# Moving the selection matrix and the combine matrix's two parts of a fused attention and soft-MoE kernel

## Chip, cores and metric

The kernel runs on one core of one Trainium2 chip. The metric is device time in microseconds (us) of one launch; lower is better. Engines are named as in the profile: PE (TensorE matmul), PEld (its weight loads), ACT (ScalarE), DVE (VectorE), POOL (GpSimd) and SP (the engine that issues the DMAs).

## What is computed

Three layers follow each other. Causal attention with a decay (4 batches, 8 heads, 576 positions, 64 per head) gives `x` of 2304 rows by 512. A soft MoE makes 32 slots out of all rows, sends them through 8 experts (4 slots each) and combines the 32 slot outputs back into rows. A second MoE of 4 experts works on all rows, weighted by given probabilities.

```python
logits = x @ phi                               # 2304 x 32
d = softmax(logits, axis=0); slot_input = d.T @ x
for e in range(8):                             # 4 slots each
    h = np.maximum(slot_input[e] @ w1[e], 0.0)
    slot_out[e] = h @ w2[e]
c = softmax(logits, axis=1)
x = c @ slot_out                               # c: the combine matrix
for e in range(4):                             # second MoE
    h = np.maximum(x @ m1[e], 0.0)
    out += p[:, e:e + 1] * (h @ m2[e])
```

## The kernel before

**Stages.** Attention runs over 16 pairs of heads to some 200 us. Then the last softmax (to 209.7), then layer one of the eight slot experts (`layer1`, L767, to 224), then layer two (`layer2`, L793, to 239), then the preparation of the second MoE (L985 to L1035), then 36 blocks of 256 rows (4 experts by 9 blocks, L1137). From L814 on the order on PE, ACT, DVE and POOL is the program's own order (`manual_schedule`); in the attention stage only PE's order is written by hand (L526) and the other engines' order is the planner's. Each engine runs its own queue in order.

**The stage in question.** `layer2_last` (L802) does the last slot expert in two halves into another bank, and DVE adds each half to `orow`, which ACT has copied out of the accumulated bank (L991, after `layer2(6)`). PE turns `orow` into `so_t` by matmuls with `i4` (L1000), DVE copies it (L1001), and `g_make` (L970) multiplies it by the first layer `m1` of expert 0 (L974). The result is split in a high and a low part (`gh`, `gl`) and `g_spread` (L883) spreads it by matmuls with `sel` into `gs`. `sel` is a constant 0/1 matrix (one wide ACT copy at L865, eight small ones at L869). `pieces` (L896) multiplies `gs` by the transposed combine matrix `c4t`; thus slot outputs and rows meet only there.

**The combine matrix.** `cn` holds the softmax of each row over the 32 slots, for 4 batches by 5 row groups. `c4_rep(b)` (L697) makes for each batch (and once for the fifth groups, b = 4) a tile `c4` of four copies: ACT rounds `cn` into `chi` (L702) and copies `chi` to places 0 and 2 (L704); POOL writes `cn - chi` to places 1 and 3 (`c4_low`, L709). PE transposes `c4` (`c4_tr`, L714) and ACT copies it to `c4t` (`c4_hi`, L719).

**The second MoE's weights.** `m2` of an expert comes as four DMAs of 512 KB into `raws`; pieces 0 and 2 early (L823), pieces 1 and 3 last (L828). Half of each 256-column tile (chunks 0 to 2) is in pieces 0 and 2, the other (chunks 2 to 4) in 1 and 3. Each tile needs a high part by ACT (`w_hi`, L757) and a low part by POOL (`w_lo`, L763): four plain ones (B00, B10, B01, B11) and four sums T1 to T4 that POOL makes first (`w_sum`, L744; T3 and T4 overwrite B01 and B00). Block 0 is done directly with the plain tiles (`direct`, L1076, L1091), after ACT and DVE have written its two parts (`hi_d` L909, `lo_d` L913, which take turns). All later blocks use seven products (`product`, L1057, L1071) with parts made by DVE, ACT and POOL (`a_sum` L960, `s_hi` L964, `s_lo` L968) and their results taken by DVE (`take`, L1052 and L1054). `PRE0` (L1111) is a table of which part is issued after which step of block 0 or 1.

**Weight buffers.** SP loads all expert weights in one fixed order (`stream`) of 512 KB pieces: 4 into `ring`, 17 into `ringb`, 14 into `ringc` (`NB`, L46), 6 in place of attention tiles, 6 into `post` (L559) and `NQ` = 4 into `post2` (L682), which lies where `xnp` and a part of `wk` (the tail of the attention, closed at L681) were. Then two pieces of `m2` once `layer1(0)` has released `ring`, four pieces of the stream after each of `layer1(1)` to `layer1(4)`, and one after `layer1(5)`, into `ringb` (L825).

Of the kernel before, what the change touches and what calls it, by code (L numbers as in the profile page):

```python
# [10 lines left out]
F32R = mybir.dt.float32r  # L11
# [23 lines left out]
def soft_moe_kernel(tc, a, out):  # L35
# [3 lines left out]
    def f32(ap):  # L39
        return ap.bitcast(F32)  # L40

    NQ = 4
    E = mybir.EngineType
    SE = [{'a': nc.scalar, 'd': nc.vector}[x] for x in "ad"]
    WU = 5
    NB = (17, 14)  # L46
    ND = 1
    with ExitStack() as top:
# [634 lines left out]

        eo = top.enter_context(tc.tile_pool(name="eo", bufs=2, side="right"))
        qx.close()

# [7 lines left out]

        c4_ps, c4_in = {}, {}

        def c4_rep(b):  # L697
            src = cn[:64, :, 4] if b == B else cn[:, b, 0:4]
            r = src.shape[0]
            c4 = c4p.tile([r, 4, 4, 32], F32, tag="c4f" if b == B else "c4", bufs=1 if b == B else 4, name=f"c4_{b}")  # L700
            chi = c4p.tile([r, 4, 32], F32R, tag="chi", bufs=5, name=f"chi_{b}")
            act.copy(chi, src)  # L702
            two_of = lambda x: x[:, :, None, :].to_broadcast([r, 4, 2, 32])
            act.copy(c4[:, :, 0:4:2], two_of(f32(chi)))  # L704
            c4_ps[b] = c4
            c4_in[b] = (c4[:, :, 1:4:2], two_of(src), two_of(f32(chi)))

        def c4_low(b):
            pool.tensor_tensor(*c4_in[b], op=ALU.subtract)  # L709

# [103 lines left out]
        man = ExitStack()  # L814
        man.enter_context(tc.manual_schedule(engines={E.PE, E.Activation, E.DVE, E.Pool}))
        for e in range(E1):
            if e == 4:
                hidden(0)
            layer1(e)
            if e == 0:  # L820
                raws[0] = ring.tile([128, 4096], F32, tag="w", name="ring_m2")
                for i in (0, 2):
                    load_w(raws[0][:, 1024 * i:1024 * i + 1024], 1, stream.index(("m2", 0, i)))  # L823
            elif e < 6:
                load_w(ringb[0], 4 if e < 5 else 1)  # L825
            if e == 5:
                for i in (1, 3):
                    load_w(raws[0][:, 1024 * i:1024 * i + 1024])  # L828
            if e == 4:
                turn(0)  # L830
                slots(0)
                slots(1)
# [12 lines left out]
        so_t = c4tp.tile([128, DC, 32], F32, name="so_t")  # L845
        sel = c4tp.tile([128, 4, 2, 128], F32R, name="sel")
        c4tp.tile([128, 8], F32, name="pad2")
# [6 lines left out]
        for x in ("T1", "T2"):  # L854
            w_sum(0, x, 0, 2)
        for x in ("B00", "B10", "B01", "B11"):
            w_hi(0, x, act, 0, 2)
            w_lo(0, x, pool, 0, 2)
        slots(5)
        layer2(5)  # L860
        w_hi(0, "T2", act, 0, 2)
        w_hi(0, "T1", act, 0, 2)
        for b in (0, 1, 2, 3, B):
            c4_rep(b)
        act.activation(sel, ident[:, None, None, 0:1].to_broadcast([128, 4, 2, 128]), AF.Copy, scale=0.0)  # L865
        for jq in range(4):
            for i in range(2):
                r = slice(32 * jq, 32 * jq + 32)
                act.copy(sel[r, jq, i, 64 * i:64 * i + 64].rearrange("p (a s) -> p a s", a=2),  # L869
                         i4[r, None, :].to_broadcast([32, 2, 32]))  # L870
        c4_low(0)
        w_sum(0, "T3", 0, 2)
        w_sum(0, "T4", 0, 2)
        c4_low(1)
        c4_low(2)
        w_lo(0, "T2", pool, 0, 2)
        c4_low(3)
        c4_low(B)
        w_lo(0, "T1", pool, 0, 2)
        slots(6)  # L880
# [105 lines left out]
        def c4_bank(b):  # L986
            return ops.tile([128, DM], F32, tag="o", name=f"ct_{b}")
# [18 lines left out]
        gg = g_make(0, bank(0, 0)[:, 0:256], range(2, DC))  # L1006
        w_hi(0, "B00", act, 2, 4)
        w_lo(0, "B00", pool, 2, 4)
        for b in (1, 2):
# [6 lines left out]
        for hf in range(2):  # L1016
            g_spread(0, *gg, hf)
        w_hi(0, "B10", act, 2, 4)
        w_lo(0, "B10", pool, 2, 4)
        c4_tr(3, c4_bank(3))  # L1020
        pieces(0, 0)
        hi_d(0, 0, 0)
        lo_d(0, 0, 0)
        hi_d(0, 0, 1)
        lo_d(0, 0, 1)
        c4_tr(B, c4_bank(B))
        pieces(0, 1)
        hi_d(0, 1, 0)
        lo_d(0, 1, 0)
        hi_d(0, 1, 1)  # L1030
        lo_d(0, 1, 1)
# [44 lines left out]
        def direct(m):  # L1076
# [3 lines left out]
            for n in range(2):  # L1080
# [29 lines left out]

        PRE0 = {(0, 0): [("hi", "B01", "a", 2, 4), ("lo", "B01", "p", 2, 4)],  # L1111
# [6 lines left out]
        ENG = {"a": act, "d": dve, "p": pool}  # L1118
# [164 lines left out]
```

## Time and profile before

| what | us |
|---|---|
| median of the runs shown (3) | 658.71 |
| lowest, highest | 657.29, 658.84 |
| the profiled execution | 658.35 |
| its span, first to last instruction | 656.6 |

PE is busy for 644.6 us of the span (98%), PEld 576.4 (88%), DVE 482.5 (73%), POOL 420.0 (64%), ACT 355.8 (54%). The mean granted TensorE clock is 0.995 of full speed. An engine's busy time is the union of its instructions; matmuls overlap, so their durations add up to more than the time they take. Idle time of an engine matters only where another one waits for it.

### The profile page before, as it was taken

Reading aid. Unit: us, or ns where it says so; the run is one execution under the profiler, and the core shown is the slowest. Engines: PE = TensorE matmul, PEld = TensorE weight load, DVE = VectorE, ACT = ScalarE, POOL = GpSimd, SP = SyncE. Lnnn points to the kernel's source line nnn. Section 1 sums busy time; section 2 is a strip of 40 time slices with the busy share of each in tenths; the row PEclk is TensorE's granted clock in tenths of the full one; section 3 lists DMA queues with packets and bytes.
Section 4 is the critical chain, followed back from the end, with each engine's and each line's share of the span. In section 5 each row is a group of like instructions: output and inputs, shape, how many; then the busy total and the mean of one; then the engine's idle time right before and its main releaser. Section 6 shows DMA issues by size and latency. Waiting matters only on the chain.

```text
span 656.6 us, 15328 instructions
## 1 busy us (share of the span) xinstructions
PE 644.6 (98%) x5646; PEld 576.4 (88%) x5646; DVE 482.5 (73%) x1330; ACT 355.8 (54%) x868; POOL 420.0 (64%) x384
## 2 busy tenths in 40 slices
PE   8999999999999989999999999999999999999998
PEld 4778788788787449899999999999999999999997
DVE  6889889888885015577678877778876778877774
ACT  7777777777772065533547343547443446444441
POOL 5677777677641195843889663789754589835443
PEclk9999999999999989999999999999999999999999
DMA  5687787787347980213000303000303000011111
GB/s 170 194 246 222 212 265 224 216 255 229 90 167 296 415 351 1 88 42 130 1 1 1 130 1 129 2 0 2 129 1 129 1 1 2 33 46 52 51 48 65
DMA packets 27510, 76.16 MB, mean 116 GB/s; under 512 B 4014, under 2 KB 4654, under 8 KB 27436
## 3 DMA queue, kind: packets, MB, share of 16 engines
q1 hardware_dynamic: 27436, 75.18, 33.9%
q8 instruction: 45, 0.74, 0.5%
q14 instruction: 29, 0.24, 0.1%
HBM read 70.31 MB, written 4.72 MB: 114 GB/s over the span
## 4 chain that ended last, share of the span: by engine, by line
PE 85%; ACT 4%; DVE 3%; POOL 3%; issue 2%; DMA 2%; ACTq 0%; DVEq 0%; POOLq 0%
PE R L1071 27%; PE Q L1071 13%; PE P L1071 7%; PE avb L290 5%; PE pt L273 5%; PE two L902 5%; PE sc L240 3%; PE sc L237 3%; PE sc L224 3%; PE pl L342 2%; PE ava L302 2%; PE pt L264 2%; DMA w<-in_w 2%; PE two L974 1%; PE nat L317 1%
## 5 line engine op out<-in xcount | busy, mean ns | idle before, releaser
L968 POOL TENSOR_TENSOR s<-S,s 128x512 fp32r<-128x512 f32 x140 | 179.8, 1320 | 131.1 <-ACT s L964 131.1
L964 ACT CAST s<-S 128x512 fp32r<-128x512 f32 x140 | 77.2, 619 | 88.7 <-PE Q L1071 51.2
L214 ACT ACTIVATE p<-p,nm 128x256 f32<-128x256 f32 (+2 forms) x144 | 83.3, 580 | 28.6 <-DVE nm L210 27.3
L1071 PE MATMUL R<-wh_T,s 128*128 128x256 f32 x560 | 88.8, 280 | 0.7 <-DVE acc L1054 0.7
L1054 DVE SCALAR_TENSOR_TENSOR acc<-R,dpn,acc 128x256 f32<-128x256 f32 x116 | 56.0, 483 | 34.6 <-PE R L1071 31.0
L934 ACT ACTIVATE a<-two 128x256 f32<-128x256 f32 x70 | 26.9, 384 | 94.9 <-PE two L902 94.5
L1071 PEld LDWEIGHTS R<-wh_T,s 128*128 128x128 f32 x560 | 75.2, 188 | 1.9 <-ACT a L943 1.2
L210 DVE CUSTOM_DVE_ANT_0 p<-sc,maskb 128x256 f32<-128x256 f32 (+2 forms) x144 | 66.9, 489 | 3.2 <-PE sc L224 1.5
L960 DVE SCALAR_TENSOR_TENSOR S<-two,S 128x256 f32<-128x256 f32 x140 | 58.9, 421 | 4.3 <-POOL s L968 1.8
L960 DVE SCALAR_TENSOR_TENSOR S<-two,a 128x256 f32<-128x256 f32 x140 | 58.1, 415 | 3.8 <-POOL s L968 2.2
L191 POOL TENSOR_TENSOR opd<-raw,opd 64x576 fp32r<-64x576 f32 x29 | 42.3, 1459 | 13.9 <-ACT opd L176 12.8
L950 DVE SCALAR_TENSOR_TENSOR q<-two,q 128x512 fp32r<-128x512 f32 x70 | 47.7, 681 | 0.0
L273 PE MATMUL pt<-ident,p 128*128 128x128 f32 x285 | 46.0, 279 | 1.3 <-ACT p L214 0.7
L902 PE MATMUL two<-c4t,gs 128*128 128x256 f32 x288 | 46.5, 284 | 0.0
L237 PE MATMUL sc<-opd 128*128 128x256 f32 (+3 forms) x128 | 46.4, 374 | 0.0
L1071 PE MATMUL Q<-wh_B,s 128*128 128x256 f32 x280 | 43.8, 278 | 1.4 <-DVE acc L1052 1.4
L1071 PE MATMUL R<-wh_T,q 128*128 128x256 f32 x280 | 44.4, 280 | 0.0
L273 PEld LDWEIGHTS pt<-ident,p 128*128 128x128 f32 x285 | 31.4, 140 | 14.8 <-issue 10.4
L1071 PE MATMUL R<-wh_B,a 128*128 128x256 f32 x280 | 44.2, 280 | 0.0
L1071 PE MATMUL R<-wl_T,s 128*128 128x256 f32 x280 | 44.1, 279 | 0.0
L1071 PE MATMUL Q<-wh_T,s 128*128 128x256 f32 x280 | 44.1, 279 | 0.0
L1071 PE MATMUL P<-wh_B,q 128*128 128x256 f32 x280 | 44.0, 279 | 0.0
(279 smaller groups left out, 1626.8 us busy)
## 6 DMA issues: line engine op xcount, KB each, us to landing
w<-in_w SPq DMA_DIRECT2D x54, 512.0 KB
ring<-in_m SPq DMA_DIRECT2D x24, 512.0 KB
raw<-in_k SPq DMA_DIRECT2D x64, 144.0 KB
v<-in_v SPq DMA_DIRECT2D x16, 320.0 KB
out<-acc SPq DMA_DIRECT2D x17, 256.0 KB
raw<-in_q SPq DMA_DIRECT2D x28, 144.0 KB
ring<-in_w SPq DMA_DIRECT2D x4, 512.0 KB
w_opd<-in_w SPq DMA_DIRECT2D x4, 512.0 KB
```

Source lines behind the costliest of these rows:

```text
L191: (dve if h == 0 else pool).tensor_tensor(lo, r, f32(hi), op=ALU.subtract)
L210: dve.tensor_tensor_reduce(out=pt_in[j][:, k0:k0 + n], in0=sc, in1=maskb[:, m0:m0 + n], scale=-SCALE, scalar=nm, op0=ALU.add, op1=ALU.min, ...
L214: act.activation(p, p, AF.Exp, bias=nm, scale=-1.0, accum_out=sums)
L237: pe.matmul(o, lhsT=qa[hh][:, qs], rhs=ka[hh][:, 0:n], start=True, stop=False)
L273: pe.transpose(t[:, i, :], pt_in[j][:, 128 * i:128 * i + 128], ident)
L902: pe.matmul(t[:, j, k], lhsT=gs[e][:, 128 * fc:128 * fc + 128], rhs=c4t[:, nb * BLK:nb * BLK + BLK])
L950: dve.scalar_tensor_tensor(o[:, 1], i, 0.0, f32(o[:, 0]), op0=ALU.max, op1=ALU.subtract)
L960: dve.scalar_tensor_tensor(sv[m, name][:, c], half[m, h][:, :, k, 128 * t:128 * t + 128], 0.0, other, op0=ALU.max, op1=op)
L964: act.copy(tile_of(m, name)[:, 0], sv[m, name])
L968: (eng or pool).tensor_tensor(o[:, 1], sv[m, name], f32(o[:, 0]), op=ALU.subtract)
L1054: dve.scalar_tensor_tensor(o, t, pcol, o, op0=ALU.mult, op1=ALU.add)
L1071: pe.matmul(t, lhsT=a[:, c, :], rhs=w[:, c, :], start=first and x == 0 and c == 0, stop=x == 2 and c == 3, skip_group_check=True)
```

## The change

`sel` and `chi` become tiles of the pool `eo`, which opens before layer one; `chi` is one tile for all batches. Ahead of the layer-one loop ACT rounds `cn` into `chi` in two copies (128 and 64 partitions) and POOL subtracts `chi` from `cn` in place, twice; ACT then makes `sel` there (L865 to L870 go). `c4_rep` becomes two ACT copies for each of its five calls, of `chi` and of the remaining `cn`; `c4_low` and its five POOL instructions go. To make room `post2` gets 2 pieces instead of 4 (`NQ`), `ringb` 19 buffers and `ringc` 12, and the load after `layer1(5)` takes 3 pieces instead of 1. In the preparation of the second MoE the high and low parts of B00, B10 and B01 (chunks 2 to 4) and the sums T1, T2 are issued at other places among the steps of block 0, and `PRE0` is shorter by what went there.

```diff
-    NQ = 4
+    NQ = 2
-    NB = (17, 14)
+    NB = (19, 12)
@@ after load_w(... "post2" ...)
         eo = top.enter_context(tc.tile_pool(name="eo", bufs=2, side="right"))
+        sel = eo.tile([128, 4, 2, 128], F32R, tag="sel", bufs=1, name="sel")
+        chi = eo.tile([128, B, 5, 32], F32R, tag="chi", bufs=1, name="chi")
@@ c4_rep
-            src = cn[:64, :, 4] if b == B else cn[:, b, 0:4]
-            r = src.shape[0]
+            src = [x[:64, :, 4] if b == B else x[:, b, 0:4] for x in (f32(chi), cn)]
+            r = src[0].shape[0]
-            chi = c4p.tile([r, 4, 32], F32R, tag="chi", bufs=5, name=f"chi_{b}")
-            act.copy(chi, src)
-            act.copy(c4[:, :, 0:4:2], two_of(f32(chi)))
+            for i in range(2):
+                act.copy(c4[:, :, i:4:2], src[i][:, :, None, :].to_broadcast([r, 4, 2, 32]))
-        def c4_low(b):
-            pool.tensor_tensor(*c4_in[b], op=ALU.subtract)
@@ ahead of the layer-one loop
+        for p, c in ((128, slice(0, 4)), (64, slice(4, 5))):
+            act.copy(chi[:p, :, c], cn[:p, :, c])
+            pool.tensor_tensor(cn[:p, :, c], cn[:p, :, c], f32(chi[:p, :, c]), op=ALU.subtract)
+        act.activation(sel, ident[:, None, None, 0:1].to_broadcast([128, 4, 2, 128]), AF.Copy, scale=0.0)
+        for jq in range(4):
+            for i in range(2):
+                act.copy(sel[...], i4[...])
@@ in the loop
-                load_w(ringb[0], 4 if e < 5 else 1)
+                load_w(ringb[0], 4 if e < 5 else 3)
@@ between layer2(4) and layer2(6)
+        for x in ("B00", "B10", "B01", "B11", "T2", "T1"):
+            w_hi(0, x, act, 0, 2)
         for x in ("B00", "B10", "B01", "B11"):
-            w_hi(0, x, act, 0, 2)
             w_lo(0, x, pool, 0, 2)
         slots(5)
         layer2(5)
-        w_hi(0, "T2", act, 0, 2)
-        w_hi(0, "T1", act, 0, 2)
         for b in (0, 1, 2, 3, B):
             c4_rep(b)
-        act.activation(sel, ...)   and the eight copies
-        c4_low(0)
-        w_sum(0, "T3", 0, 2)
-        w_sum(0, "T4", 0, 2)
-        c4_low(1)
-        c4_low(2)
-        w_lo(0, "T2", pool, 0, 2)
-        c4_low(3)
-        c4_low(B)
-        w_lo(0, "T1", pool, 0, 2)
+        for x in ("T3", "T4"):
+            w_sum(0, x, 0, 2)
+        for x in ("T2", "T1"):
+            w_lo(0, x, pool, 0, 2)
@@ preparation of block 0
-        w_hi(0, "B00", act, 2, 4)            # stood ahead of c4_tr(1)
-        w_lo(0, "B00", pool, 2, 4)
         for hf in range(2):
             g_spread(0, *gg, hf)
-        w_hi(0, "B10", act, 2, 4)
-        w_lo(0, "B10", pool, 2, 4)
+        w_sum(0, "T1", 2, 4)
+        w_hi(0, "B00", act, 2, 4)
+        w_lo(0, "B00", pool, 2, 4)
         pieces(0, 0)
         hi_d(0, 0, 0)
         lo_d(0, 0, 0)
+        w_hi(0, "B10", act, 2, 4)
+        w_lo(0, "B10", pool, 2, 4)
         hi_d(0, 0, 1)
         lo_d(0, 0, 1)
+        w_sum(0, "T2", 2, 4)
         pieces(0, 1)
         hi_d(0, 1, 0)
         lo_d(0, 1, 0)
+        w_hi(0, "B01", act, 2, 4)
+        w_lo(0, "B01", pool, 2, 4)
         hi_d(0, 1, 1)
@@ PRE0: B01 leaves it, T1 and T2 sums leave it,
-        (0, 1): B11 hi, lo, sums T1 T2;  (0, 3): sums T3 T4;  (0, 4): T2, T1 hi, lo
-        (0, 5): T3 hi;  (0, 6): T4 hi;  (1, 1): T3 lo;  (1, 2): T4 lo
+        (0, 0): B11 hi, lo, sums T3 T4;  (0, 2): T2, T1 hi, lo;  (0, 3): T3 hi, lo
+        (0, 5): T4 hi;  (1, 1): T4 lo
```

## Rows read from the trace of the kernel before

**Rows 1.** The page's 40 slices: granted TensorE clock in tenths of full.

```profile
PEclk9999999999999989999999999999999999999999
```

**Rows 2.** Waits of PE, 230 to 250 and 250 to 275 us: total, times, longest.

```profile
PE two L1000 <- DVE orow L810: 1.9, 1, 1.9
PE two L808 <- DMA w<-in_w: 0.2, 1, 0.2
...
PE Q L1071 <- DVE acc L1052: 1.4, 1, 1.4
```

**Rows 3.** Windows: length; busy of PE, PEld, DVE, ACT, POOL; PEclk; DMA share; GB/s.

```profile
240.00:241.00 1.00, 0.00 (x0) 0.00 (x0) 0.29 (x1) 0.95 (x5) 1.00 (x2) 1.00 1.02 418
241.00:242.00 1.00, 0.81 (x5) 0.82 (x6) 0.46 (x2) 1.00 (x2) 1.00 (x2) 0.76 1.02 418
245.00:246.00 1.00, 1.00 (x15) 0.39 (x8) 0.00 (x0) 0.00 (x0) 1.00 (x2) 0.50 0.00 0
...
272.00:273.00 1.00, 0.29 (x3) 0.08 (x1) 0.24 (x1) 0.00 (x0) 1.00 (x2) 1.00 0.00 0
...
275.00:400.00 125.00, 124.76 (x1088) 122.13 (x1086) 92.63 (x215) 57.52 (x119) 79.38 (x61) 1.00 0.14 52
```

**Rows 4.** Timeline of PE: start, length, instructions, idle before and what ended it.

```profile
209.69 1.93 PE L773 MATMUL two<-ring,si_f 128*32 128x256 f32 x32
...
237.82 1.49 PE L808 MATMUL two<-w,ht 128*32 128x256 f32 x20 [0.23 <-DMA w<-in_w]
...
251.61 0.28 PE L1091 MATMUL d<-wh_B,q 128*128 128x256 f32 x1
```

**Rows 5.** The chain that ended last, in order of time: start, length, what.

```profile
240.71 0.43 DVE orow L810
...
243.58 3.57 PE two L974 x32
```

**Rows 6.** Timeline of ACT, 237 to 253 us.

```profile
237.30 0.40 ACT L704 COPY c<-chi 64x256 f32<-64x256 f32 x1
237.62 1.05 ACT L865 ACTIVATE sel<-ident 128x1024 fp32r<-128x1024 f32 x1
238.70 1.58 ACT L869 CAST sel<-i 32x64 fp32r<-32x64 f32 x8
240.30 0.65 ACT L991 COPY orow<-so_ps 128x256 f32<-128x256 f32 x2
...
243.93 0.62 ACT L757 CAST wh_B<-ring_m 128x512 fp32r<-128x512 f32 x1 [0.42 <-DMA ring_m<-in_m]
...
252.12 1.09 ACT L909 ACTIVATE q<-two 128x512 fp32r<-128x512 f32 x2 [0.76 <-DVE q L913]
```

**Rows 7.** Timeline of POOL, 209 to 273 us.

```profile
209.82 0.48 POOL L671 TENSOR_TENSOR cn<-ce,cs_e 128x160 f32<-128x160 f32 x1 [5.72 <-DVE dps L672]
...
234.96 0.73 POOL L709 TENSOR_TENSOR c<-cn,chi 128x256 f32<-128x256 f32 x1
...
257.57 1.29 POOL L763 TENSOR_TENSOR wl_B<-ring_m,wh_B 128x512 fp32r<-128x512 f32 x1 [0.26 <-ACT wh_B L757]
...
272.69 1.26 POOL L763 TENSOR_TENSOR wl_T<-ring_m,wh_T 128x512 fp32r<-128x512 f32 x1
```

**Rows 8.** Timeline of DVE, just ahead of PE's wait at 273 us.

```profile
272.76 0.42 DVE L960 SCALAR_TENSOR_TENSOR S<-two,S 128x256 f32<-128x256 f32 x1 [0.81 <-POOL s L968]
273.10 0.48 DVE L1052 TENSOR_SCALAR acc<-Q,dpn 128x256 f32<-128x256 f32 x1
```

**Rows 9.** Windows as rows 3, where the weight loads pause and start again.

```profile
210.00:211.00 1.00, 1.00 (x24) 0.58 (x20) 0.74 (x4) 0.00 (x0) 0.30 (x1) 1.00 0.01 4
211.00:212.00 1.00, 1.00 (x24) 0.64 (x20) 0.00 (x0) 0.00 (x0) 0.00 (x0) 1.00 0.56 106
```

**Rows 10.** Waits of SP's DMA queue, 186 to 260 us: total, times, longest.

```profile
SPq L73 <- PE busy L661: 6.0, 1, 6.0
...
SPq L73 <- POOL cn L671: 1.1, 1, 1.1
```

More of the change, by code (lines that the diff above doesn't have):

```diff
@@ L693, in soft_moe_kernel @@
         ops = top.enter_context(tc.tile_pool(name="ops", bufs=4, space=PSUM))
-        c4_ps, c4_in = {}, {}
+        c4_ps = {}
         def c4_rep(b):
-            src = cn[:64, :, 4] if b == B else cn[:, b, 0:4]
-            r = src.shape[0]
+            src = [x[:64, :, 4] if b == B else x[:, b, 0:4] for x in (f32(chi), cn)]
+            r = src[0].shape[0]
             c4 = c4p.tile([r, 4, 4, 32], F32, tag="c4f" if b == B else "c4", bufs=1 if b == B else 4, name=f"c4_{b}")
-            chi = c4p.tile([r, 4, 32], F32R, tag="chi", bufs=5, name=f"chi_{b}")
-            act.copy(chi, src)
-            two_of = lambda x: x[:, :, None, :].to_broadcast([r, 4, 2, 32])
-            act.copy(c4[:, :, 0:4:2], two_of(f32(chi)))
+            for i in range(2):
+                act.copy(c4[:, :, i:4:2], src[i][:, :, None, :].to_broadcast([r, 4, 2, 32]))
             c4_ps[b] = c4
-            c4_in[b] = (c4[:, :, 1:4:2], two_of(src), two_of(f32(chi)))
-        def c4_low(b):
-            pool.tensor_tensor(*c4_in[b], op=ALU.subtract)
         def c4_tr(b, t):
@@ L815, in soft_moe_kernel @@
         man.enter_context(tc.manual_schedule(engines={E.PE, E.Activation, E.DVE, E.Pool}))
+        for p, c in ((128, slice(0, 4)), (64, slice(4, 5))):
[4 more added lines that the diff above has]
+            for i in range(2):
+                r = slice(32 * jq, 32 * jq + 32)
+                act.copy(sel[r, jq, i, 64 * i:64 * i + 64].rearrange("p (a s) -> p a s", a=2),
+                         i4[r, None, :].to_broadcast([32, 2, 32]))
         for e in range(E1):
@@ L845, in soft_moe_kernel @@
         so_t = c4tp.tile([128, DC, 32], F32, name="so_t")
-        sel = c4tp.tile([128, 4, 2, 128], F32R, name="sel")
         c4tp.tile([128, 8], F32, name="pad2")
@@ L860, in soft_moe_kernel @@
         layer2(5)
-        w_hi(0, "T2", act, 0, 2)
-        w_hi(0, "T1", act, 0, 2)
         for b in (0, 1, 2, 3, B):
             c4_rep(b)
[L865 to L870, printed above, removed]
-        c4_low(0)
-        w_sum(0, "T3", 0, 2)
-        w_sum(0, "T4", 0, 2)
-        c4_low(1)
-        c4_low(2)
-        w_lo(0, "T2", pool, 0, 2)
-        c4_low(3)
-        c4_low(B)
-        w_lo(0, "T1", pool, 0, 2)
+        for x in ("T3", "T4"):
+            w_sum(0, x, 0, 2)
+        for x in ("T2", "T1"):
+            w_lo(0, x, pool, 0, 2)
         slots(6)
@@ L1109, in soft_moe_kernel @@
                (9, 4): [("lo", "B11", "p", 2, 4), ("lo", "T4", "d", 0, 2)], (9, 5): [("lo", "T4", "p", 2, 4)]}
-        PRE0 = {(0, 0): [("hi", "B01", "a", 2, 4), ("lo", "B01", "p", 2, 4)],
[6 rows of a table removed]
+        PRE0 = {(0, 0): [("hi", "B11", "a", 2, 4), ("lo", "B11", "p", 2, 4), ("sum", "T3", 2, 4), ("sum", "T4", 2, 4)],
[3 rows of a table added]
         ENG = {"a": act, "d": dve, "p": pool}
```

9 rows, old and new, of the table PRE0 are left out of this document.

## The prediction, written before the change was timed

> **What bounds the kernel now.** I read the slices first. The TensorE clock is granted in full everywhere but in one slice, around 240 us [rows 1]. Next I asked for PE's waits around that place, since PE is the busiest engine: from 230 to 275 us it waits three times, 0.2 us for a weight DMA, 1.9 us for `orow` and 1.4 us for `take` [rows 2]. From 275 us on PE is busy 124.76 of 125 us [rows 3], so whatever this stretch gains before 275 us should arrive at the end undiminished. The reader is to see that only two things can be won here: the waits, and the clock.
>
> The windows show the clock. PE is idle through all of 240 to 241, and right after it the granted share is 0.76, then 0.50 [rows 3], the lower of the two levels, 1.2 GHz. What that costs is seen on matmuls of one shape: 32 of L773 take 1.93 us [rows 4], 32 of L974 take 3.57 us on the chain [rows 5]. From the first L1000 at 241.2 (the end of DVE's 240.71 + 0.43 [rows 5]) to `g_spread` at about 248.6, some 7.4 us, PE runs at about half rate.
>
> Why PE waits for `orow` is read on ACT's timeline. ACT makes `sel` from 237.62 (1.05 us and eight copies in 1.58 us), and only then, at 240.30, copies `orow` [rows 6], though PE's last `layer2_last` ends at 237.82 + 1.49 = 239.31 [rows 4].
>
> The third wait hangs on POOL. From 257.57 to 272.69 + 1.26 it works without a gap on 13 instructions of 1.26 us [rows 7]; DVE's sum waits for it and the taking of Q stands behind that sum [rows 8], and PE waits for the bank.
>
> **Part 1: `sel` and `chi` in layer one.** ACT gives up 1.05 + 1.58 = 2.63 us ahead of `orow`. `c4_rep` stays ten ACT instructions: five short casts become five copies like the 0.40 us one [rows 6], overlapping as before; I take no change, at most 0.1 us each. So the `orow` copies stand ready at 240.30 - 2.63 = 237.7, and end by 238.4 (238.9 with the dearer copies), before PE's second half ends. `post2` becomes shorter and holds nothing of the last half of expert 4, so T2's rounding may start up to a microsecond earlier; I count nothing for it. DVE's two additions (0.43 us [rows 5]) then trail the matmuls, and `c4_tr(0)` lies between the two L1000. **Gain 1.9 us**; both ends of its bound are 1.1 (a PE gap of 0.8 us is left, by the dear copies) and 1.9.
>
> What moves costs ACT 2.63 us for `sel`, and two rounding copies of `chi`; the nearest row for 512 columns is the 0.62 us of `wh_B` [rows 6], so under 1.3 us. POOL gets two subtractions, the wide one at most 1.29 us [rows 7]. They start when `cn` is ready, behind POOL's L671 at 209.82 + 0.48 = 210.3 [rows 7]. ACT's next work is `hidden(0)`, behind four experts of 1.93 us or a little less [rows 4], near 217: 6.7 us of idle time for 3.9 us of work. Nothing else waits in that queue, so it costs nothing; were the cover gone, the overhang would count only beyond the 1.9 us of the fifth expert, since `turn(0)` comes behind that.
>
> **Part 2: the clock.** With no gap of 1.9 us ahead of it the stretch should run at 2.4 GHz: half of 7.4 us, **3.7 us**, if nothing new holds PE. A shorter gap did not matter: PE is busy 0.29 of 272 to 273 and waited 1.4 us there [rows 2, 3], and the granted clock stayed at 1.00; the fall followed the one wait of 1.9 us. The Trainium skill (TensorE: Matmul & The Clock Gate, "What's actually happening") says that the throttled state is the default and activity releases it, which would let thin work alone bring the clock down; the trace speaks against it, as L773 ran at full rate at 209.69 [rows 4] in the same thin shape. By that sentence this part would bring nothing; it is the third rival.
>
> **Part 3: weight loads.** PE would now reach L974 at about 240.0, so the `m1` pieces matter. PE's 0.23 us wait ends at 237.82 with the last `w2` piece [rows 4], ACT's at 243.93 with `m2` piece 1 [rows 6], five pieces further on: 1.22 us a piece. The four `m1` pieces thus land at 239.0, 240.3, 241.5 and 242.7. PE at full rate wants them at 240.0, 240.5, 241.0 and 241.4: a new wait of 1.3 us, if loading stays as it is. But it should move. DMA is at rest from 210 to 211 [rows 9], since SP first waits 6.0 us for PE L661 and then 1.1 us for POOL's `cn` [rows 10]. Both use tiles of `wk` and `post2` lies on part of it. With half the size (8 KB a partition less, where `wk`, the outer pool, holds 8.3 KB and `post2` reached 4.3 KB into it, summing the tiles' sizes) it ends within `xnp`, which PE last reads at L648, before L661. Two pieces can then follow without a rest, until about 211.8. The two others move behind `layer1(1)`, in the same order as to all later pieces. The next loads, `m2` into `ring`, wait for `layer1(0)`, 209.69 + 1.93 = 211.6 [rows 4], and move bytes some 1.1 us later, as the load released at 210.3 [rows 7] shows by its 106 GB/s in 211 to 212 [rows 9], a quarter of the 418 of a full one [rows 3]: 212.8. Two pieces less are due then, 2 x 1.22 = 2.4 us, against a start 1.3 us later: **everything from `w2` of expert 5 on lands 1.1 us earlier.** The 0.2 us wait at L808 vanishes, and `m1`'s last piece lands at 241.6, so the new wait is 0.2 us. Bounds: 0 and 1.3 us.
>
> **Part 4: parts nearer their tiles.** ACT's roundings of B10 and B01 go between `hi_d` steps, where ACT stands idle 0.76 us for DVE [rows 6]; one takes 0.62. Free if `m2` piece 3 is there: it lands one piece behind 243.93, at 245.2, and is wanted at about 245.6 (less 1.1 us if Part 3 holds). If it is late, `hi_d(0, 0, 1)` and all of block 0 wait behind it on ACT: 0 to 0.8 us. On POOL five `c4_low` of 0.73 [rows 7] go, 3.7 us, so its parts of chunks 0 to 2 end at 243 and it is free when `m2` piece 1 lands. From there it has 16 instructions to the last part of T4 (T1, T2, T3, T4 sums, eight low parts, four `s_lo`), 16 x 1.27 = 20.3 us, and about 1.2 us of waits for ACT: it ends near 264.2, where it ended at 273.95 before: 9.7 us earlier. PE is 5.7 us earlier there (below). DVE's sum was let go at 272.76 and PE stood ready 1.44 us before 273.73; it now arrives at 272.3 - 5.7 = 266.6, later than POOL's end. **Gain 1.4 us**, bounds 0 and 1.4.
>
> **The sum.** 1.9 + 0.2 (L808) + 3.7 - 0.2 = 5.6 us up to block 0's first L1091 (251.61 [rows 4] becomes 246.0), and 1.4 behind it: 7.0 us. The profiled execution took 658.35, 0.36 below the median, with a span of 656.6 and 1.8 around it. 658.35 - 7.0 = 651.35, and with the 0.36, **651.7 us** for the median. Nothing is late next: the second MoE is bound by PE itself.
>
> **The rivals.**
> (a) Loads don't move: `post2` still waits for POOL, PE waits 1.3 us for `m1` and not 0.2, the L808 wait stays, and `hi_d` loses up to 0.4. For it: I infer which tiles lie under `post2` from sizes. 651.7 + 1.3 = 653.0, up to 653.4.
> (b) POOL's chain stays the bound of block 1, because sums now stand ahead of low parts: 1.4 us not won, 653.1.
> (c) The clock falls all the same, at `m1`'s wait or by the thin work: 3.4 to 3.7 us not won, 655.3. Against it: a gap of 1.4 us did nothing at 272 us.
> (d) The change doesn't do what it says: ACT is held elsewhere ahead of `orow` (T2's rounding waits for a weight buffer until later), the 1.9 us gap and the low clock stay and only Part 4 pays, 657.3.
> (e) Slower. In the attention stage only PE's order is written by hand; the planner orders ACT, DVE and POOL, and the two pools whose sizes change open there. If it lays the stage out otherwise, each of 16 head pairs can lose. It decides from 7.0 / 16 = 0.44 us a pair on; with 0.6 us a pair the time is 651.7 + 9.6 = 661.3. Against it: the same instructions and the same number of loads are issued there, and the buffers are only shared out otherwise.
>
> **How the numbers follow.** Chances: forecast 0.58, (a) 0.14, (b) 0.08, (c) 0.09, (d) 0.06, (e) 0.05. The predicted time is 651.7. The forecast alone holds 650.6 to 652.9 by its bounds (the low end 1.1 us under, if T2's earlier rounding and the loads bring more). To leave out no more than 2 in 10 the range takes in (a) and (b) and reaches to (c): 650.4 to 655.4. About 0.3% (2 us) is what a measurement of this kernel can tell from no change. Faster by more than that: forecast, (a), (b), (c), 0.89; within it (d), 0.06; slower (e), 0.05.
>
> **What would show it.** Right: PEclk without a dip around 240 us; PE's wait for `orow` gone; 32 L974 in under 2.5 us; the first L1091 near 246; traffic in 210 to 211; no PE wait on L1052 near 266. Wrong: a new PE wait at L974 for `m<-in_m` over 1 us (a), the wait on L1052 still there (b), a granted 0.50 anywhere (c), ACT idle ahead of `wh_T` and `orow` copies still at 240 (d), or the end of attention later than 209 us (e).

## The result, and the profile after

| what | kernel before, us | changed kernel, us |
|---|---|---|
| median (4 runs each, same chip) | 658.78 | 652.58 |
| lowest to highest | 657.29 to 659.28 | 652.29 to 653.07 |
| the profiled execution | 658.35 | 652.6 |
| its span | 656.6 | 650.8 |

The changed kernel is faster: the ratio is 0.991, with an interval of 0.9893 to 0.9928, or 6.2 us between the medians. The prediction said 651.7, within 650.4 to 655.4. The forecast case came, 0.9 us short. That the number is so near is in part luck: the runs below show that several of its terms had the wrong size, and that these errors partly cancel.

Lines move in the changed kernel: L773 becomes L769, L808 L804, L1000 L992, L974 L966, L1091 L1087, L1071 L1067, L991 L983, L968 L960.

The page of the changed kernel (span; the granted clock in 40 slices) has no slice below 9, where [rows 1] had an 8:

```profile
span 650.8 us, 15329 instructions
...
PEclk9999999999999999999999999999999999999999
```

The waits of PE from 10 to 275 us (total, times, longest). Both large waits of [rows 2] are gone, and so is the 0.2 us at the last layer two. New are 0.4 us for `m1` and 0.9 us for a load in the attention stage, of which the prediction said nothing; the lines left out here stand in the kernel before too, within 0.2 us:

```profile
PE ava L302 <- DMA v<-in_v: 0.9, 1, 0.9
...
PE two L966 <- DMA m<-in_m: 0.4, 1, 0.4
```

The windows (columns as in [rows 3]). The weight loads move 381 GB/s through 210 to 211, where [rows 9] show 4. PE is busy through 240 to 242 at full clock, where [rows 3] show an empty microsecond and then half rate. The dip of 0.44 us in 242 to 243 is the wait for `m1`, and the clock stays at 1.00:

```profile
210.00:211.00 1.00, 0.94 (x13) 0.67 (x16) 0.87 (x6) 0.00 (x0) 0.19 (x1) 1.00 1.11 381
...
240.00:241.00 1.00, 1.00 (x13) 0.91 (x15) 0.35 (x3) 0.47 (x1) 1.00 (x2) 1.00 1.05 430
241.00:242.00 1.00, 1.00 (x24) 0.50 (x16) 0.12 (x1) 0.12 (x1) 1.00 (x1) 1.00 1.01 414
242.00:243.00 1.00, 0.56 (x16) 0.16 (x8) 0.00 (x0) 0.00 (x0) 1.00 (x2) 1.00 1.04 426
```

The timeline of PE (columns as in [rows 4]). Layer one begins at 210.69, 1.0 us later than before; the first direct matmul comes at 247.50 instead of 251.61:

```profile
210.69 1.93 PE L769 MATMUL two<-ring,si_f 128*32 128x256 f32 x32
...
237.55 1.91 PE L804 MATMUL two<-w,ht 128*32 128x256 f32 x32
239.39 0.63 PE L992 MATMUL two<-i,orow 128*128 128x32 f32 x4
...
240.79 1.50 PE L966 MATMUL two<-m,so_t 128*32 128x256 f32 x24
...
242.74 0.64 PE L966 MATMUL two<-m,so_t 128*32 128x256 f32 x8 [0.44 <-DMA m<-in_m]
...
247.50 0.28 PE L1087 MATMUL d<-wh_B,q 128*128 128x256 f32 x1
```

The timeline of ACT. `sel` is made at 212.05 to 214.7, and ACT then still waits 3.15 us for PE, so the move is hidden. The `orow` copies start at 237.86, 2.4 us earlier than in [rows 6], and 3.4 us earlier counted from the start of layer one:

```profile
212.05 1.05 ACT L815 ACTIVATE sel<-ident 128x1024 fp32r<-128x1024 f32 x1
213.13 1.59 ACT L819 CAST sel<-i 32x64 fp32r<-32x64 f32 x8
...
217.87 0.38 ACT L775 ACTIVATE hr<-two 128x256 f32<-128x256 f32 x1 [3.15 <-PE two L769]
...
237.86 0.65 ACT L983 COPY orow<-so_ps 128x256 f32<-128x256 f32 x2
```

**Where the time went, stretch by stretch.** Four marks from PE's timelines split each profiled execution: the start of layer one, the first product with `orow` (`two<-i,orow`), the first direct matmul (`d<-wh_B,q`), and the first Q matmul with `wh_B` of block 1, which is where PE waited 1.44 us before (273.73). The columns in the middle are differences of these starts. In the kernel before, the second mark is this line:

```profile
241.19 0.79 PE L1000 MATMUL two<-i,orow 128*128 128x32 f32 x4 [1.88 <-DVE orow L810]
```

| kernel (described below) | layer one starts | to first `orow` product | from there to first direct | from there to Q | span |
|---|---|---|---|---|---|
| before | 209.69 | 31.50 | 10.42 | 22.12 | 656.6 |
| changed | 210.69 | 28.70 | 8.11 | 20.11 | 650.8 |
| changed, second profile | 210.65 | 28.71 | 8.25 | 20.10 | 650.7 |
| changed, third profile | 210.70 | 28.70 | 7.91 | 20.09 | 650.4 |
| gap filled (own bank) | 209.95 | 31.49 | 7.44 | 22.11 | 654.4 |
| loads only | 210.00 | 30.63 | 9.08 | 22.11 | 655.1 |
| order only | 211.08 | 31.50 | 9.08 | 20.11 | 655.0 |
| changed, old order | 210.06 | 28.71 | 8.24 | 22.14 | 652.0 |
| changed, `sel` late | 209.94 | 30.52 | 7.45 | 20.10 | 650.8 |
| changed, combine parts late | 209.95 | 28.70 | 7.96 | 20.54 | 651.2 |
| changed, two `v` buffers | 210.34 | 28.71 | 7.85 | 20.11 | 649.8 |

For the changed kernel: 2.8 us won up to the first `orow` product (predicted 1.9 + 0.2), 2.3 from there to the first direct matmul (predicted 3.7 - 0.2), 2.0 behind it (predicted 1.4), 1.0 lost ahead of layer one (not foreseen) and 0.3 lost after the last mark: 5.8 us, the difference of the two spans.

### The profile page after: what moved, and what is told of

Same layout as the page of the kernel before. It is cut to its first block, busy times and chain, and to the rows that moved or that the text cites. A ratio compares the mean times of both kernels' runs of the same rounds, so it can differ in the third digit from the quotient of the medians.

```text
span 650.8 us, 15329 instructions
## 1 busy us (share of the span) xinstructions
PE 641.3 (99%) x5646; PEld 574.9 (88%) x5646; DVE 483.0 (74%) x1330; ACT 356.7 (55%) x870; POOL 418.5 (64%) x381
## 4 chain that ended last, share of the span: by engine, by line
PE 89%; DVE 3%; DMA 3%; ACT 2%; issue 1%; ACTq 0%; DVEq 0%
PE R L1067 28%; PE Q L1067 14%; PE P L1067 7%; PE avb L290 5%; PE pt L273 5%; PE two L894 5%; PE sc L240 3%; PE sc L237 3%; PE sc L224 3%; PE pl L342 2%; PE ava L302 2%; PE pt L264 2%; PE d L1087 2%; DMA m<-in_m 2%; PE two L769 1%
## 5 line engine op out<-in xcount | busy, mean ns | idle before, releaser
L960 POOL TENSOR_TENSOR s<-S,s 128x512 fp32r<-128x512 f32 x140 | 180.0, 1321 | 133.4 <-ACT s L956 133.4
L1067 PE MATMUL R<-wh_T,s 128*128 128x256 f32 x560 | 88.7, 280 | 0.7 <-DVE acc L1050 0.7
L1067 PEld LDWEIGHTS R<-wh_T,s 128*128 128x128 f32 x560 | 75.3, 188 | 1.5 <-ACT a L935 1.2
L1067 PE MATMUL R<-wh_T,q 128*128 128x256 f32 x280 | 44.6, 281 | 0.0
L1067 PE MATMUL R<-wh_B,a 128*128 128x256 f32 x280 | 44.3, 280 | 0.0
L1067 PE MATMUL Q<-wh_T,s 128*128 128x256 f32 x280 | 44.1, 279 | 0.0
L1067 PE MATMUL R<-wl_T,s 128*128 128x256 f32 x280 | 44.1, 279 | 0.0
L1067 PE MATMUL P<-wh_B,q 128*128 128x256 f32 x280 | 44.1, 279 | 0.0
L1067 PE MATMUL Q<-wh_B,s 128*128 128x256 f32 x280 | 43.8, 278 | 0.0
```

Source lines behind the costliest of these rows:

```text
L960: (eng or pool).tensor_tensor(o[:, 1], sv[m, name], f32(o[:, 0]), op=ALU.subtract)
L1067: pe.matmul(t, lhsT=a[:, c, :], rhs=w[:, c, :], start=first and x == 0 and c == 0, stop=x == 2 and c == 3, skip_group_check=True)
```

## The experiments

Each job ran its kernels on one chip beside the kernel before. The before medians of the three jobs are 657.39, 657.53 and 657.52 us (22, 23 and 10 executions), and in each case a ratio goes against its own job's.

### Was it the gap that brought the clock down? A first filling

The kernel before, with dummy identity matmuls on PE where it waits for `orow`:

```diff
+        for _ in range(7): pe.matmul(bank(0, 0)[:, 0:128], lhsT=ident, rhs=ident)
```

> The kernel before, with seven dummy matmuls of the identity into a free bank between the last `layer2_last` matmul and the first L1000, some 1.65 us of PE work; the wait for `orow` itself stays. Theory (the 1.9 us gap is what the clock fell after): the granted clock stays at 1.00 around 240 us, 32 L974 take about 1.9 us and not 3.57, the first L1091 comes 3.7 us earlier, and the median goes from 658.8 to 655.1. Rival (the thin work brings the clock down, or the fall has nothing to do with the gap): a granted 0.50 still follows at about 241 us, and the time stays within 0.5 us of 658.8.

Measured 659.46 us, ratio 1.0032 (1.0017 to 1.0048). The waits of PE and its timeline say why it does not test the gap: the bank that I filled is in the tile that DVE was still to read for `orow`, so the fillers themselves stood in the wait that they were to fill, and then added their own time.

```profile
PE two L998 <- DVE orow L810: 2.0, 1, 2.0
```

```profile
242.30 2.55 PE L998 MATMUL two<-ident 128*128 128x128 f32 x14 [1.98 <-DVE orow L810]
```

One thing it does show. The gap is left, but behind it now stand 128x128 fillers and not the thin products (32 columns of weights or of input); the clock falls all the same, while the fillers run (window, columns as in [rows 3]):

```profile
243.00:244.00 1.00, 1.00 (x9) 1.00 (x7) 0.00 (x0) 0.00 (x0) 1.00 (x1) 0.61 1.01 414
```

### The same in a bank of its own

```diff
+        dum = c4_bank("dum")
+        for _ in range(7): pe.matmul(dum[:, 0:128], lhsT=ident, rhs=ident)
```

> The kernel before with the seven dummy matmuls again, now into a bank that DVE doesn't read, so that they run while PE waits for `orow`. Theory (the gap of about 1.9 us is what lets the clock fall, in more than half of the executions): every execution has a granted clock of 0.999 or 1.0, and the time is that of the executions of the kernel before with such a clock, about 1.7 us below those at 0.997, or 1.3 us below the median of the kernel before. Rival (thin work alone lets the clock fall): clocks of 0.995 and 0.997 stay as frequent as in the kernel before, and the median is within 0.4 us of it.

Measured 656.2 us (655.44 to 657.09), ratio 0.9983 (0.9969 to 0.9997). Of PE's waits from 230 to 275 us the one for `orow` is gone, while the two others are left:

```profile
PE Q L1074 <- DVE acc L1055: 1.4, 1, 1.4
PE two L808 <- DMA w<-in_w: 0.4, 1, 0.4
```

PE's timeline has the fillers in the gap, and 32 matmuls with `m1` behind it take 1.93 us, against 3.57 in [rows 5]:

```profile
239.69 1.83 PE L999 MATMUL ct_dum<-ident 128*128 128x128 f32 x14
241.44 0.63 PE L1003 MATMUL two<-i,orow 128*128 128x32 f32 x4
...
242.84 1.93 PE L974 MATMUL two<-m,so_t 128*32 128x256 f32 x32
...
248.88 0.28 PE L1094 MATMUL d<-wh_B,q 128*128 128x256 f32 x1
```

The window that was empty in [rows 3] is full, at full clock:

```profile
240.00:241.00 1.00, 1.00 (x11) 1.00 (x10) 0.04 (x1) 0.96 (x5) 1.00 (x2) 1.00 1.02 418
```

So the idle gap is what the clock falls after: nothing else was changed, no work was saved, and the kernel gained. What the fall costs is the surprise. The mean granted clock of every execution is known. Of 55 executions of the kernel before, 33 have 0.997 or less (median 657.93) and 22 have 0.999 or 1.000 (median 656.09); of the 11 with the filled gap none is below 0.999. So the clock fell in about 60% of the executions and cost 1.8 us when it did; the kernel with the gap filled beats the one with the gap by 1.3 us in the median. The execution that I had read, with a half rate of 6.8 us and a mean of 0.995, was a dear one. In the profiled executions of the first filling and of the runs with the loads alone and the order alone (below) the half rate lasts 3.4 us, half as long, after waits of 1.8 to 2.0 us.

The table prices both. The same work from the first `orow` product to the first direct matmul takes 7.44 us at full clock, 9.08 with 3.4 us of half rate and 10.42 with 6.8 us: 1.6 and 3.0 us for one fall. (A mean of 0.997 can come from elsewhere too: in one profile of the changed kernel it comes from a dip in the warm-up at 10.9 to 14.3 us. In the kernels of this document that have no wait for `orow`, 3 of 50 executions have 0.997 or less. So the 60% is an upper estimate of how often it fell here, by a few per cent.)

### `sel` back behind `c4_rep`

The changed kernel with ACT's nine `sel` instructions where they stood before:

```diff
-        act.activation(sel, ...)      # ahead of the layer-one loop, and its eight copies
         ...
         for b in (0, 1, 2, 3, B):
             c4_rep(b)
+        act.activation(sel, ...)      # and its eight copies
```

> The changed kernel, with the making of `sel` (2.63 us of ACT) put back behind `c4_rep`, ahead of the `orow` copies; buffers, `chi` and the order of the parts stay as changed. Theory: PE waits about 1.9 us for `orow` again, the clock falls again, and the time is 4.5 to 5.6 us above that of the changed kernel (652.6), 657.1 to 658.2; PE's wait for the `m1` load disappears, since PE is later than it. Rival (only the wait itself matters, the clock's fall was chance): 1.5 us above, 654.1. Second rival (`chi`, not `sel`, was what freed ACT): no more than 0.3 us above.

Measured 653.65 us, ratio 0.9947 (0.9931 to 0.9964), so 1.4 to 2.4 us above the changed kernel (ratios 0.9910, 0.9919 and 0.9926 in three jobs), not the 4.5 us and more that my theory gave. The wait of PE, its timeline (the wait is between these two lines), and the `orow` copies on ACT's timeline:

```profile
PE two L992 <- DVE orow L806: 1.0, 1, 1.0
```

```profile
236.81 2.65 PE L804 MATMUL two<-w,ht 128*32 128x256 f32 x32
240.46 0.63 PE L992 MATMUL two<-i,orow 128*128 128x32 f32 x4 [1.00 <-DVE orow L806]
```

```profile
239.58 0.65 ACT L983 COPY orow<-so_ps 128x256 f32<-128x256 f32 x2
```

The wait is back, at half its length, for two reasons. With the other edits in place the same ACT queue reaches `orow` 1.0 us earlier, counted from layer one (29.64 us after its start, before 30.61). And PE itself was late in this execution: its last 32 products of layer two took 2.65 us instead of 1.91. So the wait understates what `sel`'s place is worth; the table's marks give it. With `sel` late the first `orow` product comes 1.8 us later than in the changed kernel (30.52 against 28.70), and 0.7 us of that comes back behind it, since PE then no longer waits for `m1` (7.45 against 8.11): 1.2 us up to the first direct matmul.

The clock was below 0.999 in 3 of 6 executions (median 654.39, against 653.51 of the others). The profiled one is not among them, so that it fell after this wait is not shown. Beside the other edits, `sel`'s move saves 1.2 us, and possibly the clock in some executions.

### The loads alone

The kernel before with the new sharing of the weight buffers and nothing else:

```diff
-    NQ = 4
+    NQ = 2
-    NB = (17, 14)
+    NB = (19, 12)
-                load_w(ringb[0], 4 if e < 5 else 1)
+                load_w(ringb[0], 4 if e < 5 else 3)
```

> The kernel before with the buffer sizes and the loads alone changed (`NQ`, `NB`, three pieces after `layer1(5)`); `sel`, `chi` and all parts stay. Theory: SP no longer waits for POOL's L671, DMA traffic goes on through the microsecond in which it rested, later pieces land about 1.1 us earlier, PE's 0.2 to 0.5 us wait at L808 goes, and the time is 0.2 to 0.5 us below the kernel before: hardly to be told from it. Rival (the order of the pieces costs more than the rest gives): up to 1 us above. If the wait for `v` in attention comes from the buffer sizes, layer one starts 1 us later here too.

Measured 656.31 us, ratio 0.9984 (0.9971 to 0.9998): 0.9 us between executions of like clock (655.2 against 656.1, and 657.0 against 658.0). I had counted 0.2 us for what vanishes at L808. The gain is on ACT, which PE waits for:

```profile
232.84 1.14 ACT L757 CAST wh_T<-T 128x512 fp32r<-128x512 f32 x2 [1.30 <-POOL wl_B L763]
...
239.75 0.65 ACT L991 COPY orow<-so_ps 128x256 f32<-128x256 f32 x2
```

In the kernel before this rounding of T2 starts at 233.38 after 2.16 us of waiting, and the copies at 240.30 [rows 6]. Layer one starts 0.31 us later here, so T2's rounding comes 0.85 us earlier and all that stands behind it in ACT's queue too, `sel` and `orow` among it. PE's first `orow` product follows, 30.63 us after the start of layer one instead of 31.50:

```profile
236.87 1.91 PE L808 MATMUL two<-w,ht 128*32 128x256 f32 x32
240.63 0.63 PE L1000 MATMUL two<-i,orow 128*128 128x32 f32 x4 [1.85 <-DVE orow L810]
```

Its wait is no shorter (1.85 us, before 1.88), since PE gets there earlier as well: without the wait for `w` its last 32 products of layer two take 1.91 us, before 2.75. (The other 1.3 us by which this profile is ahead at the first direct matmul are the shorter half rate, 9.08 against 10.42.) That the rounding moves is shown; that it moves because `post2`, half as long, no longer covers the last weights that layer two of expert 4 reads is read from the tiles' sizes, and no run tests it by itself. It is the microsecond for which the prediction counted nothing.

### The order of the parts alone

The kernel before, with the order of `w_hi`, `w_lo` and `w_sum` and the table `PRE0` of the changed kernel:

```diff
-        w_hi(0, "B00", act, 2, 4)        # ahead of c4_tr(1)
-        w_lo(0, "B00", pool, 2, 4)
         ...                              # T1, T2 sums, B00, B10, B01 among
+        w_sum(0, "T1", 2, 4)             # the steps of block 0, as in the change
```

> The kernel before, with nothing changed but the places of the parts of B00, B10, B01, B11 and T1 to T4 (chunks 2 to 4) and the shorter table; `sel`, `chi`, the five POOL subtractions and the buffers stay as before. Theory (POOL's chain into block 1 is shortened by the order): the 1.4 us wait of PE on L1052 at 272 us goes and the rest stays, 657.3. Rival (the order is worth nothing while POOL has the five subtractions to do first): 658.8, and the wait is still above 1 us.

Measured 655.39 us, ratio 0.9975 (0.9962 to 0.9989). The wait for `take` is gone with POOL's five `c4_low` still in place, and from the first direct matmul to Q it takes 20.11 us, exactly as in the changed kernel:

```profile
PE two L1000 <- DVE orow L810: 1.8, 1, 1.8
PE two L808 <- DMA w<-in_w: 0.3, 1, 0.3
```

### The change without the new order

The reverse: the changed kernel with the order of the parts as before.

> The changed kernel with the parts' places and the table of before; `sel`, `chi`, `c4_rep` and the buffers stay as changed. Theory (the order pays the last term): B01's and B11's low parts go late again and POOL's chain, which then ends near 268.4 where PE is ready at 267.4, holds PE for 1.2 to 1.7 us at the same product of block 1: 653.8 to 654.3. Rival (the five POOL subtractions that went pay it): the wait stays away and the time is within 0.3 us of the changed kernel's 652.6.

Measured 654.14 us, ratio 0.9955 (0.9939 to 0.997). The wait is back in full, and the stretch takes 22.14 us, as before:

```profile
PE Q L1063 <- DVE acc L1044: 1.4, 1, 1.4
PE two L966 <- DMA m<-in_m: 0.3, 1, 0.3
```

POOL shows how, though its `c4_low` are gone here. A low part waits 4.21 us (in the kernel before just as long, in the changed one no such wait is above 1.14 us) for ACT's high part, which stands late in ACT's queue, and all sums stand behind it, so the last `s_lo` of block 1 ends at 268.2:

```profile
251.42 1.30 POOL L759 TENSOR_TENSOR wl_B<-ring_m,wh_B 128x512 fp32r<-128x512 f32 x1 [4.21 <-ACT wh_B L753]
...
265.63 2.53 POOL L960 TENSOR_TENSOR s<-S,s 128x512 fp32r<-128x512 f32 x2
```

In the changed kernel the same two instructions end at 265.8, on an execution whose layer one starts 0.63 us later:

```profile
263.17 2.59 POOL L960 TENSOR_TENSOR s<-S,s 128x512 fp32r<-128x512 f32 x2
```

Both runs together: the order is worth 2.0 us (22.1 against 20.1, with and without every other edit). POOL's relief without the order gives none of it.

### The combine matrix's parts as before

The changed kernel, with `chi` rounded in `c4_rep` and five `c4_low` on POOL again; `sel`, order and buffers stay changed:

```diff
-            act.copy(chi[:p, :, c], cn[:p, :, c])          # ahead of layer one
-            pool.tensor_tensor(cn[...], cn[...], f32(chi[...]), op=ALU.subtract)
+            act.copy(chi, src)                             # in c4_rep
+        c4_low(0) ... c4_low(B)
```

> The changed kernel with the combine matrix's parts made as before: ACT rounds each batch in `c4_rep`, POOL does its five `c4_low`; `sel` stays early, the order of the parts and the buffers stay as changed. Theory after the last runs (the parts' order alone ends the wait in block 1, and POOL has room for 3.7 us more): within 0.4 us of the changed kernel, no PE wait on DVE's `take` in block 1. Rival (my prediction's reason, POOL's freedom is part of the 1.4 us): 0.5 to 1.5 us above, with some of that wait back.

Measured 652.2 us, ratio 0.9925 (0.9911 to 0.994); the changed kernel ran in the same job at 652.22 and 0.9926 (0.991 to 0.9942). A small piece of the old wait is there:

```profile
PE two L973 <- DMA m<-in_m: 0.3, 1, 0.3
PE Q L1074 <- DVE acc L1055: 0.3, 1, 0.3
```

So the early combine parts save 0.4 us from the first direct matmul to Q (20.54 against 20.11), and the total shows no difference. The part of the change that rewrites `c4_rep` brings nothing that can be measured in the total.

### Work of block 0 put into the wait for `m1`

The changed kernel with one of PE's transposes of the combine matrix moved ahead of the last quarter of the `m1` product:

```diff
-        gg = g_make(0, ..., range(2, DC))
+        g_make(0, ..., range(2, 3))
+        c4_tr(1, c4_bank(1)); c4_hi(1)
+        gg = g_make(0, ..., range(3, DC))
```

> The changed kernel with `c4_tr(1)` moved ahead of the last quarter of `g_make`, into PE's 0.3 to 0.4 us wait for the last `m1` piece. Theory (that wait is on the path): the wait at L966 goes, block 0 starts 0.3 to 0.4 us earlier, and so does the end: 0.3 to 0.4 us below the changed kernel. Rival (what PE did behind `g_make` covered DVE's split in `gh` and `gl`): PE now waits as long for `gh`, and nothing is gained.

Measured 651.77 us, ratio 0.9932 (0.9914 to 0.995); the changed kernel in the same job 651.54 and 0.9919 (0.9904 to 0.9934). No gain. The wait for `m1` is not in the list, and another of the same length stands in its place, for the split of that product by DVE into `gh` and `gl`:

```profile
PE two L879 <- DVE gl L973: 0.4, 1, 0.4
```

The transposes had covered this split. The 0.4 us only changes its name.

### Two buffers for `v`

The changed kernel with a second `v` buffer, and the load issued earlier, at the first half of the pair before:

```diff
-    vp = ...bufs=1
+    vp = ...bufs=2
-    load_v(pr + 1)     # in av_b, i == 2
+    load_v(pr + 1)     # in av_a, i == 0
```

> The changed kernel with two buffers for `v` instead of one and its load issued one pair of heads earlier, at the first half of the pair before, so that no slow load can reach the matmuls. Theory (the wait of 0.3 to 1.1 us for `v` near 91 us, seen in four of nine traces whatever the buffers of the weights, is a transfer that sometimes comes late): that wait is gone and the median is 0.2 to 0.6 us below the changed kernel. Rival (the early load pushes the other loads of attention back): other DMA waits of as much come up, no gain or up to 1 us above.

Measured 651.64 us (651.44 to 652.46), ratio 0.9917 (0.9903 to 0.9931). The wait for `v` is gone from the list of PE's waits ahead of 210 us; another load, of `opd`, was late instead:

```profile
PE pt L264 <- ACT p L214: 1.1, 2, 0.6
...
PE sc L240 <- DMA opd<-opd: 0.3, 1, 0.3
```

It is 0.6 us below the changed kernel's 652.22 in the same job, but the intervals overlap, and the unchanged kernel had 651.54 in another job, so it isn't shown to be faster.

### The changed kernel again

It ran once more in each of the two later jobs, as the measure of the others:

> The changed kernel once more, unedited, for a second trace of its attention stage and for times on the same chip as the next three. If the 0.9 us that PE waited for a `v` load at 91 us in its first trace belongs to the new buffer sizes, it stands here again at the same place; if it is chance, layer one starts near 209.7 us as in the kernel before, the span is about 1.0 us shorter (649.8), and the time lies 5.5 to 6.5 us below the kernel before. The granted clock is 0.999 or 1.0 in every execution.

Measured 651.54 us (651.26 to 652.45), ratio 0.9919.

> The changed kernel, unedited, as the base on this chip for the next two. Expected 651.3 to 652.8, and 5.5 to 6.5 us below the kernel before; a PE wait of 0 to 1 us for `v` in the attention stage, differing from execution to execution.

Measured 652.22 us (651.82 to 653.38), ratio 0.9926. PE's wait for `v` is 0.9 us in the first profile of this kernel, 0.6 and 0.2 in these two; in the second it does not stand at the same place but one pair of heads later, at 103.4 us instead of 92. Layer one starts at 210.65 and 210.70, as late as in the first profile: the `ava` products also begin later than in the kernel before (20.46), at 20.84 in the second and, behind the dip of the clock in the warm-up, at 21.21 in the third. The wait shows up in five of the twelve traces with one `v` buffer, with the old and the new buffer sizes (1.1 in the run with the order alone, 0.3 with the transpose moved), and not in the kernel before, nor with the loads alone, nor with `sel`, the order or the combine parts put back. The kernel with `sel` late has the same tiles in attention as the changed one and no such wait. A load that lands late by chance fits all of them; a cost of the new buffers doesn't. But all four traces of the whole change show the wait, and one of the other eight, so a cause in the program as a whole is not excluded. The traces don't show what makes the load late.

## Why the prediction was right or wrong

**Part 1, the wait for `orow`: right, and worth more than its 1.9 us.** The wait is gone, the moved work is hidden (ACT waits 3.15 us behind it), and `sel` put back brings a wait again. With the wait at L808 the sum had 2.1 us up to the first `orow` product; 2.8 came. A wait in the list is idle time alone: before, the 32 L808 products around the listed 0.2 us take 2.75 us (236.56 to 239.31), now 1.91:

```profile
236.56 1.03 PE L808 MATMUL two<-w,ht 128*32 128x256 f32 x12
```

That `sel` put back costs 1.8 us at this mark and not 2.8 is due to Part 3: ACT's queue is 1.0 us earlier without it.

**Part 2, the clock: right in cause, wrong in size.** "With no gap of 1.9 us ahead of it the stretch should run at 2.4 GHz" holds: the filled gap keeps the clock at 1.00 with no other change. The term of 3.7 us is the mis-sized one, twice over. In the very execution that I had read the fall cost 3.0 us (10.42 against 7.44): "half of 7.4 us" takes the whole stretch as one at half rate that halves, but 6.8 us were at half rate, and not all of the work in them took twice its time. And the median of the runs is not that execution: the fall comes in some 6 of 10, costs 1.8 us each, and is worth 1.3 us in the median. The step that failed is "half of 7.4 us" taken for the median too, with 0.36 us added as if the profiled execution were an ordinary one. That a gap of 1.4 us does nothing is borne out: the filled gap and the old order keep PE's wait of 1.4 us in block 1, and all 17 executions of the two have a clock of 0.999 or 1.0.

Rival (c), that the clock falls all the same, fell: neither the wait of 0.4 us for `m1` nor the thin 128x32 products of layers one and two lowered it in the changed kernel's first profile. By these rows the clock stayed at 1.00 through the 30 us from 210.69 to 241, which are nearly all such thin products. The Trainium skill (TensorE: Matmul & The Clock Gate, "What's actually happening") calls the throttled state the default that activity releases; the thin work here did not bring that state back.

**Part 3, the loads: right in direction, one step missed.** In the waits of SP's queue from 186 to 260 us the two of [rows 10] (6.0 us for PE's L661, 1.1 for POOL's `cn`) are no longer there, but two shorter ones for earlier instructions of the tail of attention:

```profile
SPq L73 <- PE fin_c L652: 3.0, 1, 3.0
...
SPq L73 <- DVE xn L620: 2.2, 1, 2.2
```

The loads run through 210 to 211, and the wait at L808 is gone. The new wait for `m1` is 0.4 us (predicted 0.2, bounds 0 to 1.3), and with the slower products around it it costs 0.7 (8.11 against 7.44). "T2's rounding may start up to a microsecond earlier; I count nothing for it" is the step that failed: it starts 0.85 us earlier and ends PE's wait for `orow` by as much earlier where that wait still stands, which is how the loads alone gain 0.9 us. In the full change this overlaps Part 1, since the wait is gone anyhow, so it costs the sum nothing.

**Part 4, the order: right in place, wrong in reason and size.** PE's wait on the taking of Q is gone, as said. I gave the credit to POOL's 3.7 us of removed subtractions together with the order. The order alone does it; the subtractions bring 0.4 us of that stretch beside the other edits, and nothing measurable in the total. The gain is 2.0 us rather than 1.4, since the wait listed is only part of what the late parts cost: on PE's timelines the three groups of products just ahead of it start up to 0.62 us apart in the kernel before and 0.47 apart in the changed one. The roundings put among the `hi_d` steps were free, as said: the whole 0.7 us between the changed kernel and the filled gap up to the first direct matmul is at `m1`.

**The sum.** For the pair of profiled executions 5.6 + 1.4 was predicted and 5.1 + 2.0 came. The medians hold less clock. Between executions at full clock the changed kernel gains 4.6 us in the second job (656.1 to 651.5) and 4.0 in the third (656.1 to 652.1). The traces at full clock give 2.1 us to the first direct matmul (31.49 + 7.44 of the filled gap less 28.70 + 8.11) and 2.0 behind it, 4.1 us. The falls of the clock add 1.4 in either job (before medians of 657.5 against 656.1); with them the changed kernel gains 6.0 us in the second job and 5.3 in the third, where two of its six executions have 0.997. The 6.2 of the first measurement is the largest of the three, with only four executions of the kernel before, all of them longer than the longest at full clock in the later jobs (656.82).

So the prediction's 7.0 was too high. The clock term was some 2.3 us too large and the new wait for `m1` 0.5 too small; the order term, 0.6 too small, and the terms up to the first `orow` product, 0.7 too small, gave part of that back. Each of these sizes is read from a run; that the number came within 0.9 us is owed to this, and to a first measurement in which the kernel before was dear.

**What was not seen.** Attention ends 1.0 us later in the profiled execution of the changed kernel, which is what I had named as the mark of rival (e). It isn't that: PE's `avb` products show the loss in one place, 12.28 us from the sixth pair's (80.51) to the seventh's (92.79) where the kernel before takes 11.34, and no loss in the pairs around it. That is the late `v`. The profiles with parts of the change put back (old order, `sel` late, combine parts late) start layer one at 209.9 to 210.1; the two further ones of the changed kernel start it at 210.65 and 210.70, for the reasons given there.

## What to carry to other kernels

A dip of the clock in one profile is priced by the granted clocks of many executions, not by the one that shows it; filling the gap with idle work in a bank of its own measures it directly. A wait in the list is not the price of its cause: compare the starts of the same two instructions in both traces (a listed 0.2 us was part of 0.8, a listed 1.4 part of 2.0). When a pool gets shorter, list everything that is laid under its end, the work of another engine's queue too, not only the transfers that were meant. Where an engine's last result is late, look for an instruction in its queue that waits for a late partner before counting its amount of work: moving the high parts, low parts and sums to other places in their queues was worth 2.0 us, and taking five subtractions off the same engine 0.4 at most.

## What the runs showed of the hardware

- After one PE wait of 1.9 us the granted clock fell to the lower level in about 60% of the executions and stayed there for 6.8 us in one profile; in three others, after waits of 1.8 to 2.0 us, it stayed there for 3.4 us. One such fall cost 3.0 and 1.6 us. In no profile did it fall after the wait of 1.4 us near 273 us, and with 14 passes of dummy matmuls in the gap it fell in none of 11 executions.
- A load of `v` in the same program makes PE wait 0.9, 0.6 and 0.2 us in three executions, and not always at the same pair of heads; over twelve traces of nearly the same attention stage the wait is between nothing and 1.1 us. Beside differences of half a microsecond this noise must be looked up in each trace.
